# The last tile's h as seven products of halves over two of three row blocks, and its third token block ahead of the seven products of g

## The chip, the cores and the metric

The kernel runs on one core of a Trainium2 chip. The metric is device time in microseconds of one execution, from several executions. One execution was also recorded by the hardware profiler; the profile and the trace below are of that one.

The names of the engines are those of the profile. PE is TensorE's matmul and PEld its loading of weights; DVE is VectorE, ACT ScalarE, POOL GpSimd, SP the engine that issues most transfers. Every engine works through its own queue in order and waits at an instruction until the semaphores it names have come.

## What is computed

A recurrent attention (RWKV6) over 4 batches, 8 heads, 768 positions and 48 channels, whose output is taken as 3072 tokens of 384 channels, and then a feed-forward block with exact gelu:

```
for t in range(S):
    cur = einsum('bhd,bhe->bhde', u * k_t, v_t)
    y[:, :, t] = einsum('bhd,bhde->bhe', r_t, state + cur)
    state = w_t[..., None] * state + einsum('bhd,bhe->bhde', k_t, v_t)

x = y as (3072, 384)
h = x @ w_in              # w_in  (384, 2048)
g = 0.5 * h * (1 + erf(h / sqrt(2)))
out = g @ w_out           # w_out (2048, 384)
```

All is fp32. The change concerns only the feed-forward block, and of it the last 384 tokens.

## The kernel before

**Tiles.** The 3072 tokens are eight tiles of T = 384, numbered x = 0 to 7. For each, `attention(x, ...)` makes `xT`, the tile's input with channels on the partitions (three row blocks of 128 channels, 384 tokens wide), and `mlp(x)` makes the output from it. Both are generators: each `yield` is a step. The main loop runs the steps of `mlp(x - 1)` and, at steps listed by hand in `place` and `place_next`, lets the attention of tile x go on; `times` lists the steps at which loads are issued, and `more` is a generator of extra vector work of which each step takes one part. Instructions stand on each engine's queue in the order in which the code issues them. After the loop, `mlp(7)` runs alone: no attention, no load and no other step is beside it.

**h.** In `mlp`, for each of the 16 blocks f of 128 columns of `w_in`, three matmuls (L726), one for each row block j, add up a 128 x 384 block of h in a PSUM tile `h_ps`, of which there are two in turn. ScalarE applies gelu (L729) and writes the block into a `g` tile in SBUF. Where `waits` holds (x = 1, 3, 5), the last 128 tokens go into `alone` instead (L731).

**The output.** For x > 0 (`halves`) the order of the groups of f is 0, 2, 1, 3. The first two token blocks of 128 are done by seven products of halves: g over two token blocks and two halves of f, `w_out` over two halves of f and two of its columns, so that eight products of 128 x 1024 by 1024 x 192 become seven. The sums of `w_out` are made once by `w_sums` (`sums`), those of g in the last group of f by VectorE (L739, L740, L741: `s1`, `s2`, `s3`). Each product is eight matmuls of 192 columns (L746) into one of two PSUM tiles in turn, `o1` and `o2`; ScalarE or VectorE empties each (L777 to L807). The third token block of an odd tile waits in `alone` and is done with the third block of the next even tile, likewise by seven products (L816 to L851). The last tile, x = 7, has no next one, so its third block is done plainly, 16 matmuls of 384 columns (L860), after its seven products:

```python
            for blocks in ((2,),) if halves else ((0, 1), (2,)):
                o_ps = [ps.tile([128, BANK], F32, name="o_ps", tag="mm", bufs=2)[:, 0:DM] for _ in blocks]
```

VectorE copies it (L866) and SP stores it.

**PSUM.** `h_ps`, `o_ps` and `warm` share the tag "mm", two tiles of one bank. The attention has the tag "d": three tiles `[128, 2, BANK]`, each of two banks of 512 fp32.

**The attention beside it.** In tiles x >= 2 it begins with chains on VectorE (L339 to L390); then `quarters` lays out copies of r (`plain` by ScalarE, L488; `lay_out` by VectorE, L493 and L494), which 48 small matmuls read (L508, then L515). It does so twice, for 4 and for 16. Then come the states (L610, L615), the outputs `y_ps` (L630, L648) and the copies into `xT` (L672, L679). The buffers `kx`, `tot_sb`, `bufs[0]`, `bufs[1]` and `v_in` that the change uses again belong to this part.

Of the kernel before, what the change touches and what calls it, by code (L numbers as in the profile page):

```python
# [10 lines left out]
F32 = mybir.dt.float32  # L11
# [5 lines left out]
AF = mybir.ActivationFunctionType  # L17
# [6 lines left out]
T = 384  # L24
# [7 lines left out]
BANK = 512  # L32
# [12 lines left out]
def kernel(  # L45
# [25 lines left out]
    nc = tc.nc  # L71
    NX = rkw.shape[0]
    NP = u.shape[1]
    NPART = NP // Q
    N_TOK, DM = out.shape
    HALVES = 2
    NJ = DM // 128
    DF = w_in.shape[1]
    NF = DF // 128
# [4 lines left out]
    io = ctx.enter_context(tc.tile_pool(name="io", bufs=2))  # L84
    wk = ctx.enter_context(tc.tile_pool(name="wk", bufs=2))
    cv = ctx.enter_context(tc.tile_pool(name="cv", bufs=HALFWAY))
    gp = ctx.enter_context(tc.tile_pool(name="gp", bufs=4))
    ps = ctx.enter_context(tc.tile_pool(name="ps", bufs=1, space=PSUM))
# [11 lines left out]
    bufs = [io.tile([128, 3 * NP * T], F32, name=f"rkw{i}", bufs=1) for i in range(2)]  # L100
    ALL = NP * T
# [46 lines left out]
    w_out_sb = const.tile([128, NF, DM], F32, name="w_out_sb")  # L148

    WI = PIECE // NJ  # L150
    FP = PIECE // DM
    FI = WI // 128
    w_in_sb = const.tile([128, DF // WI, NJ, WI], F32, name="w_in_sb")
# [68 lines left out]
    kx = const.tile([128, 2 * NPART * NI * 3 * C // 2], F32, name="kx")  # L222
# [7 lines left out]
    for i, h in enumerate(QUARTERS):  # L230
        for a in range(3):
            w_q = (3 - a) * C // 4
            z = q_ints[1 if a == 0 else 2]
            o = i * C if a < 2 else i * C + C // 2
# [26 lines left out]
    tot_sb = const.tile([128, NP * T], F32, name="tot_sb")  # L261
# [50 lines left out]
    xT_of = {}  # L312
# [372 lines left out]
    HF, HM = NF // 2, DM // 2  # L685
    FG = 4
    sums, s3_sb = [], []
# [4 lines left out]
    def w_sums():  # L692
# [3 lines left out]
        for i, (x, y) in enumerate((((0, 1), (0, 0)), ((1, 1), 0), ((1, 1), (0, 1)), ((1, 0), 1))):  # L696
            for k in range(2):
                ks = slice(k * FG, (k + 1) * FG)
                nc.vector.tensor_sub(sums[i][:, ks], w_quarter(*x, k), sums[y][:, ks] if isinstance(y, int) else w_quarter(*y, k))
                yield  # L700

    def mlp(x):

        xT = xT_of.pop(x)
        halves = x > 0
        waits, ends = x % 2 == 1 and x < NX - 1, x % 2 == 0 and x > 0
        gs = {}
# [7 lines left out]
        def new_sums(tag):  # L717
            return cv.tile([128, FG, 128], F32, name="s", tag=tag)

        s1, s2, s3 = [], [], []  # L720
        for n, group in enumerate((0, 2, 1, 3) if halves else range(4)):
            gs[group] = gp.tile([128, FG, T], F32, name="g")
            for f in range(group * FG, (group + 1) * FG):
                h_ps = ps.tile([128, BANK], F32, name="h_ps", tag="mm", bufs=2)[:, 0:T]
                for j in range(NJ):
                    nc.tensor.matmul(h_ps, lhsT=w_in_sb[:, f // FI, j, f % FI * 128:(f % FI + 1) * 128], rhs=xT[:, j, :],  # L726
                                     start=(j == 0), stop=(j == NJ - 1))
                t = T - 128 if waits else T
                nc.scalar.activation(out=gs[group][:, f % FG, 0:t], in_=h_ps[:, 0:t], func=AF.Gelu)  # L729
                if waits:  # L730
                    nc.scalar.activation(out=alone[:, f], in_=h_ps[:, t:], func=AF.Gelu)  # L731

                if halves and n == 3 and f % FG >= FG - 2:
                    k = f % FG - FG + 2
                    for s, tag in ((s1, "f"), (s2, "e")):
                        s.append(new_sums(tag))
                    s3.append(s3_sb[0][:, k * FG:(k + 1) * FG])
                    a00, a10, a11 = (gs[g][:, :, a:a + 128] for g, a in ((k, 0), (k, 128), (k + 2, 128)))
                    nc.vector.tensor_add(s1[k], a10, a11)  # L739
                    nc.vector.tensor_sub(s2[k], s1[k], a00)  # L740
                    nc.vector.tensor_sub(s3[k], a00, a10)  # L741
                yield

        def product(o, lhs, rhs, start=False):
            for j in range(HF):
                nc.tensor.matmul(o, lhsT=lhs(j), rhs=rhs(j), start=start and j == 0, stop=(j == HF - 1),  # L746
                                 skip_group_check=True)
# [10 lines left out]
        def of_alone(b):  # L758
            return lambda j: alone[:, b * HF + j]
# [4 lines left out]
        def psum():  # L764
            return ps.tile([128, BANK], F32, name="o_ps", tag="mm", bufs=2)[:, 0:HM]

        def two_rows():
            return [wk.tile([128, DM], F32, name="o_sb", bufs=2) for _ in range(2)]


        if halves:
            row0 = x * T
            o_sb = two_rows()
            p1, u2, u3 = (wk.tile([128, HM], F32, name=name, bufs=1) for name in ("p1", "u2", "u3"))
# [21 lines left out]
            for c in range(2):  # L796
                z = o_sb[1][:, c * HM:(c + 1) * HM]
                nc.vector.tensor_add(z, z, u3)
            store(row0 + 128, o_sb[1])
            if ends:  # L800
                s1 = [new_sums("f") for k in range(2)]
# [7 lines left out]
            if ends:  # L809
                s2 = [new_sums("e") for k in range(2)]  # L810
# [5 lines left out]
        if waits:  # L816
            _, o2, o1 = psum(), psum(), psum()
            o_sb = wk.tile([128, DM], F32, name="o_sb", bufs=2)
            product(o2, of_alone(0), of_w(0, 0), True)
            nc.scalar.copy(out=p1_alone, in_=o2)  # L820
            yield
            product(o1, of_alone(1), of_w(1, 0), True)
            nc.vector.tensor_add(o_sb[:, 0:HM], o1, p1_alone)
            store(row0 + 256, o_sb[:, 0:HM])
            yield
        elif ends:
            o_sb = two_rows()
            p1, u2, u3 = p1_alone, *(wk.tile([128, HM], F32, name=name, bufs=1) for name in ("u2", "u3"))
            o2, o1 = psum(), psum()
            product(o1, of_blocks(2, 1), of_t(3), True)  # L830
            nc.scalar.copy(out=o_sb[1][:, 0:HM], in_=o1)
            yield
            product(o2, of_sums(s2), of_t(1), True)
            nc.vector.tensor_add(u2, o2, p1)
            yield
            product(o1, of_sums(s1), of_t(0), True)
            nc.scalar.copy(out=o_sb[1][:, HM:], in_=o1)
            for k in range(2):
                nc.vector.tensor_sub(s2[k], alone[:, HF + k * FG:HF + (k + 1) * FG], s2[k])
            yield  # L840
            product(o2, of_sums(s3), of_t(2))
            nc.vector.tensor_add(u3, o2, p1)
            for c in range(2):
                z = o_sb[1][:, c * HM:(c + 1) * HM]
                nc.vector.tensor_add(z, z, u3)
            store(row0 + 256, o_sb[1])
            yield
            product(o1, of_sums(s2), of_w(1, 1))
            nc.vector.tensor_add(o_sb[0][:, 0:HM], o1, u2)
            store(row0 - T + 256, o_sb[0][:, 0:HM], HM)  # L850
            yield  # L851
        else:

            if halves:
                psum()
            for blocks in ((2,),) if halves else ((0, 1), (2,)):
                o_ps = [ps.tile([128, BANK], F32, name="o_ps", tag="mm", bufs=2)[:, 0:DM] for _ in blocks]
                for f in range(NF):
                    for i, o in zip(blocks, o_ps):
                        nc.tensor.matmul(o, lhsT=block(i, f // HF, f % HF), rhs=w_out_sb[:, f, :],  # L860
                                         start=(f == 0), stop=(f == NF - 1))
                    if (not halves or f % 4 == 3) and f < NF - 1:
                        yield
                for i, o in zip(blocks, o_ps):
                    o_sb = wk.tile([128, DM], F32, name="o_sb", bufs=2)
                    nc.vector.tensor_copy(out=o_sb, in_=o)  # L866
                    store(x * T + i * 128, o_sb)
                yield
# [35 lines left out]
    for x in range(1, NX):  # L904

        place = [1, 3, 5, 7, 9, 11, 13, 15, 18, 20, 26, 32] if x == 1 else [1, 6, 8, 13, 15, 16, 18, 18, 20, 21]
        place_next = [38, 47] if x == 1 else [21, 24] if x % 2 == 0 else [25, 27]
        loads = load(x + 1, nc.scalar if x > 1 else nc.sync)

        times = range(20, 30) if x == 1 else (2, 3, 4, 5, 16, 17, 18, 19, 20, 21)  # L910
        following = attention(x + 1, 0) if x + 1 < NX else iter(())
        more = iter(())
        for step, _ in enumerate(mlp(x - 1)):
            if x == 1 and step == 2 * NF - 2:

                make_quarter_masks()
                more = w_sums()
            next(more, None)
            if x == 1 and step in (0, 2, 4, 6, 8, 10, 12, 14, 15, 17, 18, 20, 22, 24):
                convert()  # L920
            if step in times:
                next(loads, None)
            while place and place[0] <= step:
                place.pop(0)
                next(slots, None)
            while place_next and place_next[0] <= step:
                place_next.pop(0)
                next(following, None)
        for _ in slots:
            pass  # L930
        slots = following
# [62 lines left out]
```

## Time and profile before

| | us |
|---|---|
| executions | 611.08, 608.43, 612.21; median 611.08 |
| profiled execution, own time | 609.14 |
| its span, first to last instruction | 607.3 |

The last tile's `mlp` takes the last 63 us of the span. From the trace:

| part of the last tile | engine, line | records | us each |
|---|---|---|---|
| h | PE L726, 384 columns | 96 | 0.49 |
| gelu | ACT L729, 384 columns | 16 | 0.49 |
| sums of g | DVE L739 to L741, 512 columns | 6 | 0.69 |
| seven products | PE L746, 192 columns | 112 | 0.33 |
| adds from PSUM | DVE L786, L795, L807, 192 columns | 3 | 0.36 |
| copies from PSUM | ACT L777, L780, L783, L789, 192 columns | 4 | 0.32 |
| third block | PE L860, 384 columns | 32 | 0.49 |

How to read it: a matmul of the code appears as two records. A record is longer than the distance to the next, since matmuls are pipelined, so times of many are taken from the chain of waits, and not from count times mean. "Idle before" is time in which an engine stood still ahead of a group, with the instruction that ended it.

### The profile page before, as it was taken

What the parts mean: (1) busy time and instruction counts of PE and PEld (TensorE: products, weight loads), DVE (VectorE), ACT (ScalarE), POOL (GpSimd) and SP (SyncE); (2) the same over time, 40 slices, a digit from 0 to 9 for tenths busy, and PEclk for the clock granted to TensorE, in tenths of its full rate; (3) what the DMA queues carried; (4) which work ended last, traced back from release to release, by engine and by line L of the source; (5) the groups of instructions that cost most, each with busy time, mean ns of one, the idle gap of its engine ahead of it and who ended that gap; (6) DMA issues with size and microseconds to landing.
All of it is one profiled execution on the core that took longest, in us unless ns stands there. A gap on an engine that the chain in (4) does not pass through costs nothing.

```text
span 607.3 us, 15828 instructions
## 1 busy us (share of the span) xinstructions
PE 594.4 (98%) x6934; PEld 445.9 (73%) x6934; DVE 448.5 (74%) x801; ACT 173.4 (29%) x389; POOL 8.4 (1%) x24
## 2 busy tenths in 40 slices
PE   8879999999999999999999999999999999999997
PEld 4556666556698569986699568986699568995694
DVE  8969999998875978588885988679785988520120
ACT  2346376023222322213222232213222232112200
POOL 3100000000000000000000000000000000000000
PEclk9999999999999999999999999999999999999999
DMA  5767358012042305203052304203052002010001
GB/s 198 244 205 229 107 158 301 32 35 77 12 103 76 91 2 109 73 21 92 1 111 73 98 1 89 86 28 91 3 111 71 8 2 40 22 37 0 1 1 40
DMA packets 50565, 46.71 MB, mean 77 GB/s; under 512 B 31680, under 2 KB 35904, under 8 KB 50496
## 3 DMA queue, kind: packets, MB, share of 16 engines
q1 hardware_dynamic: 33152, 29.31, 15.8%
q10 hardware_dynamic: 17344, 16.39, 9.9%
q8 instruction: 55, 0.90, 0.6%
q14 instruction: 14, 0.11, 0.1%
HBM read 36.24 MB, written 4.72 MB: 67 GB/s over the span
## 4 chain that ended last, share of the span: by engine, by line
PE 86%; DVE 10%; issue 2%; ACT 1%; DVEq 0%
PE h_ps L726 37%; PE o_ps L746 31%; PE d L515 4%; PE o_ps L860 4%; DVE rkw L437 2%; PE kv_ps L592 2%; PE y_ps L648 2%; DVE e L306 2%; PE y_ps L630 2%; PE d L402 2%; PE warm L190 2%; DVE w_out_sb L310 1%; DVE a_sb L447 1%; PE d L508 1%; DVE f L303 1%
## 5 line engine op out<-in xcount | busy, mean ns | idle before, releaser
L726 PE MATMUL h_ps<-xT,w_in_sb 128*128 128x384 f32 x768 | 254.1, 489 | 1.4 <-ACT f L291 1.4
L726 PEld LDWEIGHTS h_ps<-xT,w_in_sb 128*128 128x128 f32 x768 | 144.1, 190 | 98.5 <-ACT f L291 1.9
L729 ACT ACTIVATE g<-h_ps 128x384 f32<-128x384 f32 (+1 forms) x128 | 57.3, 449 | 197.9 <-PE h_ps L726 197.9
L746 PE MATMUL o_ps<-t,s 128*128 128x192 f32 x480 | 81.9, 329 | 0.0
L746 PEld LDWEIGHTS o_ps<-t,s 128*128 128x128 f32 x480 | 77.8, 190 | 0.7
L546 DVE COPY_PREDICATED a_sb<-quarter,d 128x384 f32<-128x384 uint8 (+2 forms) x108 | 45.0, 438 | 2.5
L860 PE MATMUL o_ps<-w_out_sb,g 128*128 128x384 f32 x128 | 43.2, 491 | 0.2
L746 PE MATMUL o_ps<-w_out_sb,g 128*128 128x192 f32 x224 | 38.7, 326 | 0.0
L746 PEld LDWEIGHTS o_ps<-w_out_sb,g 128*128 128x128 f32 x224 | 37.0, 190 | 1.9
L860 PEld LDWEIGHTS o_ps<-w_out_sb,g 128*128 128x128 f32 x128 | 23.7, 190 | 17.1 <-DVE w_out_sb L310 1.4
L739 DVE TENSOR_TENSOR s<-g 128x512 f32<-128x512 f32 x14 | 9.4, 670 | 29.1 <-ACT g L729 29.1
L746 PE MATMUL o_ps<-w_out_sb,s 128*128 128x192 f32 x160 | 28.3, 330 | 0.0
L746 PE MATMUL o_ps<-t,g 128*128 128x192 f32 x160 | 27.6, 326 | 0.0
L402 PEld LDWEIGHTS d<-rkw 64*64 64x64 f32 x1152 | 18.6, 134 | 12.1 <-DVE rkw L437 7.4
L339 DVE TRANSPOSE_TENSOR_REDUCE rkw<-kx 128x48 f32<-128x1536 f32 (+3 forms) x24 | 26.8, 1154 | 0.2
L515 PEld LDWEIGHTS d<-kx,rkw 64*64 64x64 f32 x1152 | 24.3, 133 | 3.4 <-DVE a_sb L553 1.6
L515 PE MATMUL d<-kx,rkw 64*64 64x96 f32 x1152 | 26.5, 245 | 0.0
L746 PEld LDWEIGHTS o_ps<-t,g 128*128 128x128 f32 x160 | 26.3, 190 | 0.0
L746 PEld LDWEIGHTS o_ps<-w_out_sb,s 128*128 128x128 f32 x160 | 25.9, 190 | 0.4
L528 DVE TENSOR_TENSOR rkw<-rkw,tot_sb 128x768 f32<-128x768 f32 x12 | 11.5, 958 | 17.5 <-PE d L515 17.5
L402 PE MATMUL d<-rkw 64*64 64x64 f32 (+1 forms) x1152 | 21.0, 221 | 3.2 <-DVE rkw L437 2.3
L375 DVE TENSOR_TENSOR rkw<-rkw 128x384 f32<-128x384 f32 (+2 forms) x24 | 23.6, 1002 | 0.4
(117 smaller groups left out, 645.1 us busy)
## 6 DMA issues: line engine op xcount, KB each, us to landing
rkw<-in_rkw_dram ACTq DMA_DIRECT2D x45, 256.0 KB, 2.8
raw<-in_w_out_dram SPq DMA_DIRECT2D x8, 768.0 KB, 4.4
out_dram<-o_sb SPq DMA_DIRECT2D x21, 192.0 KB, 1.9
raw<-in_w_in_dram SPq DMA_DIRECT2D x5, 768.0 KB, 5.9
v_in<-in_v_dram ACTq DMA_DIRECT2D x5, 584.0 KB, 3.7
raw<-in_w_in_dram SPq DMA_DIRECT2D x9, 256.0 KB, 3.4
rkw<-in_rkw_dram SPq DMA_DIRECT2D x8, 288.0 KB, 3.9
rkw<-in_rkw_dram SPq DMA_DIRECT2D x9, 256.0 KB, 7.3
```

The source lines that it names most:

```text
L190: nc.tensor.matmul(t, lhsT=zeros[:, 0:128], rhs=zeros, start=True, stop=True)
L306: nc.vector.scalar_tensor_tensor(out=e, in0=hi, scalar=0x80000000, in1=e, op0=ALU.bitwise_and, op1=ALU.bitwise_or)
L339: nc.vector.tensor_reduce(out=fine_sb[:, e, 0:n].rearrange("p a n -> p (a n)"), in_=kx[:, o:o + n * n_m].rearrange("p (m j) -> p m j", j=3 ...
L375: nc.vector.tensor_mul(z, z, by)
L402: nc.tensor.matmul(d[half[p], g, n * width:(n + 1) * width], lhsT=kc[half[g], b, i, p], rhs=right(half[g], b, i, p), start=True, stop=True)
L437: nc.vector.tensor_mul(rk, rk, tt)
L515: nc.tensor.matmul(d[half[p], g, i * 3 * C // 2:(i + 1) * 3 * C // 2], lhsT=kc[half[g], (n + i) // NI, (n + i) % NI, p], rhs=rx[half[g], 2 ...
L546: nc.vector.copy_predicated(out=an[:, :, :, :, (a + 1) * h:], mask=mask.to_broadcast(data.shape), data=data)
L726: nc.tensor.matmul(h_ps, lhsT=w_in_sb[:, f // FI, j, f % FI * 128:(f % FI + 1) * 128], rhs=xT[:, j, :], start=(j == 0), stop=(j == NJ - 1))
L729: nc.scalar.activation(out=gs[group][:, f % FG, 0:t], in_=h_ps[:, 0:t], func=AF.Gelu)
L746: nc.tensor.matmul(o, lhsT=lhs(j), rhs=rhs(j), start=start and j == 0, stop=(j == HF - 1), skip_group_check=True)
L860: nc.tensor.matmul(o, lhsT=block(i, f // HF, f % HF), rhs=w_out_sb[:, f, :], start=(f == 0), stop=(f == NF - 1))
```

## The change

For the last tile alone, three things are different.

1. **h by seven products.** A generator `h_sums` makes four sums of `w_in` (`in_s`, each 128 x 1024, in two halves of 512) and four differences of `xT` (`in_t`, each 128 x 192), on VectorE, in the steps 2, 3, 4, 5, 17, 19, 22, 23, 24 and 26 of `mlp(6)`. They lie in buffers that the attention no longer needs: `bufs[0]`, a `v_in` buffer, `kx`, `bufs[1]`, `tot_sb`. Then `h_halves` makes the blocks f and f + 8 of h together, over two token halves of 192 and the first two row blocks, by seven products of 128 x 128 by 128 x 192; the third row block is added plainly, four matmuls of 192. Six PSUM accumulators lie in the three "d" tiles, one in each bank. VectorE puts the results together (`u2`, `u3`, `u5`, `c12`, `c21`, `c22`), and ScalarE's gelu writes four pieces of 192.
2. **The sums of g** (now `of_g`, one operation a step) are spread over the following pairs.
3. **The third token block** comes ahead of the seven products, with the blocks f = 7 and 15 last, and ScalarE copies it.

Tiles 0 to 6 issue the same instructions as before, apart from the ten steps of `h_sums`.

```diff
+    def h_sums():
+        n = DF // 2
+        rest = io.tile([128, v.shape[2]], F32, name="v_in")
+        for z in (bufs[0][:, 0:n], rest[:, 0:n], kx[:, 0:n], bufs[1][:, ALL:ALL + n]):
+            in_s.append(z.rearrange("p (i c) -> p i c", c=WI))
...
+        for i in range(4):
+            for k in range(2):
+                if i == 0:
+                    nc.vector.tensor_add(s(1, k), w(1, 0, k), w(1, 1, k))
+                elif i == 1:
+                    nc.vector.tensor_sub(s(2, k), s(1, k), w(0, 0, k))
+                elif i == 2:
+                    nc.vector.tensor_sub(s(3, k), w(0, 0, k), w(1, 0, k))
+                else:
+                    nc.vector.tensor_sub(s(4, k), w(0, 1, k), s(2, k))
+                yield
+        in_t.extend(tot_sb[:, i * HT:(i + 1) * HT] for i in range(4))
...
+        nc.vector.tensor_sub(in_t[0], x01, x00)
+        nc.vector.tensor_sub(in_t[1], x11, in_t[0])
+        yield
+        nc.vector.tensor_sub(in_t[2], x11, x01)
+        nc.vector.tensor_sub(in_t[3], x10, in_t[1])
+        yield
...
+        def h_halves():
+            banks = [ps.tile([128, 2, BANK], F32, name="d", tag="d", bufs=3) for _ in range(3)]
+            b_1, b_6, b_7, b_5, b_4, b_0 = (z[:, i, 0:HT] for z in banks for i in range(2))
...
+                multiply(b_1, (w(0, 0), x00))
+                nc.scalar.copy(out=p1, in_=b_1)
+                multiply(b_6, (s(2), in_t[1]))
+                nc.vector.tensor_add(u2, b_6, p1)
+                multiply(b_7, (s(3), in_t[2]))
+                nc.vector.tensor_add(u3, b_7, u2)
+                multiply(b_5, (s(1), in_t[0]))
+                nc.vector.tensor_add(u5, b_5, u3)
+                multiply(b_1, (w(0, 1), x10), (w(0, 2), last[0]), start=False)
+                gelu(0, 0, b_1)
+                multiply(b_4, (w(1, 1), in_t[3]), (w(1, 2), last[0]))
+                nc.vector.tensor_add(c21, b_4, u3)
+                gelu(1, 0, c21)
+                multiply(b_0, (w(1, 2), last[1]))
+                nc.vector.tensor_add(c22, b_0, u5)
+                gelu(1, 1, c22)
+                multiply(b_5, (s(4), x11), (w(0, 2), last[1]), start=False)
+                nc.vector.tensor_add(c12, b_5, u2)
+                gelu(0, 1, c12)
+                next(more, None)
+                if f % FG == FG - 1:
+                    more = of_g(k)
...
+        if final:
+            o_ps = ps.tile([128, BANK], F32, name="o_ps", tag="mm", bufs=2)[:, 0:DM]
+            order = [f for f in range(NF) if f % HF < HF - 1] + [HF - 1, NF - 1]
+            for n, f in enumerate(order):
+                nc.tensor.matmul(o_ps, lhsT=block(2, f // HF, f % HF), rhs=w_out_sb[:, f, :], start=(n == 0), stop=(n == NF - 1))
+            o_sb = wk.tile([128, DM], F32, name="o_sb", bufs=2)
+            nc.scalar.copy(out=o_sb, in_=o_ps)
+            store(x * T + 256, o_sb)
+            yield
...
-        else:
-
-            if halves:
-                psum()
-            for blocks in ((2,),) if halves else ((0, 1), (2,)):
+        elif not final:
+
+            for blocks in (0, 1), (2,):
...
-            next(more, None)
+            if x == NX - 1 and step == 2:
+                more = h_sums()
+            if x < NX - 1 or step in (2, 3, 4, 5, 17, 19, 22, 23, 24, 26):
+                next(more, None)
```

`multiply` issues one matmul for each pair of factors into the same accumulator, the first of them overwriting unless `start=False`; `gelu(a, b, z)` writes row half a and token half b of the pair's block of g.

More of the change, by code (lines that the diff above doesn't have):

```diff
@@ L700, in w_sums, with w, s @@
                 yield
+    HT = T // 2
+    in_s, in_t = [], []
+    def h_sums():
[3 more added lines that the diff above has]
+            in_s.append(z.rearrange("p (i c) -> p i c", c=WI))
+        hi = DF // WI // 2
+        def w(a, c, k):
+            return w_in_sb[:, a * hi + k * hi // 2:a * hi + (k + 1) * hi // 2, c, :]
+        def s(i, k):
+            return in_s[i - 1][:, k * hi // 2:(k + 1) * hi // 2]
+        for i in range(4):
[10 more added lines that the diff above has]
+        in_t.extend(tot_sb[:, i * HT:(i + 1) * HT] for i in range(4))
+        xT = xT_of[NX - 1]
+        x00, x01, x10, x11 = (xT[:, c, b * HT:(b + 1) * HT] for c in range(2) for b in range(2))
+        nc.vector.tensor_sub(in_t[0], x01, x00)
[4 more added lines that the diff above has]
+        yield
     def mlp(x):
@@ L718, in new_sums, with of_g @@
             return cv.tile([128, FG, 128], F32, name="s", tag=tag)
+        def of_g(k):
+            for s, tag in ((s1, "f"), (s2, "e")):
+                s.append(new_sums(tag))
+            s3.append(s3_sb[0][:, k * FG:(k + 1) * FG])
+            a00, a10, a11 = (gs[g][:, :, a:a + 128] for g, a in ((k, 0), (k, 128), (k + 2, 128)))
+            nc.vector.tensor_add(s1[k], a10, a11)
+            yield
+            nc.vector.tensor_sub(s2[k], s1[k], a00)
+            yield
+            nc.vector.tensor_sub(s3[k], a00, a10)
+            yield
@@ new lines, in h_halves, with w, s, multiply @@
+        def h_halves():
+            banks = [ps.tile([128, 2, BANK], F32, name="d", tag="d", bufs=3) for _ in range(3)]
+            b_1, b_6, b_7, b_5, b_4, b_0 = (z[:, i, 0:HT] for z in banks for i in range(2))
+            temps = [bufs[1][:, 2 * ALL + i * HT:2 * ALL + (i + 1) * HT] for i in range(8)]
+            x00, x01, x10, x11 = (xT[:, c, b * HT:(b + 1) * HT] for c in range(2) for b in range(2))
+            more = iter(())
+            for f in range(HF):
+                k = f // FG
+                if f % FG == 0:
+                    for group in (k, k + 2):
+                        gs[group] = gp.tile([128, FG, T], F32, name="g")
+                p1, u2, u3 = (wk.tile([128, HT], F32, name=name, bufs=1) for name in ("p1", "u2", "u3"))
+                u5, c12, c21, c22 = temps[f % 2::2]
+                def w(a, j):
+                    g = a * HF + f
+                    return w_in_sb[:, g // FI, j, g % FI * 128:(g % FI + 1) * 128]
+                def s(i):
+                    return in_s[i - 1][:, f // FI, f % FI * 128:(f % FI + 1) * 128]
+                def multiply(o, *factors, start=True):
+                    for i, (lhsT, rhs) in enumerate(factors):
+                        nc.tensor.matmul(o, lhsT=lhsT, rhs=rhs, start=start and i == 0, stop=(i == len(factors) - 1),
+                                         skip_group_check=True)
+                def gelu(a, b, z):
+                    nc.scalar.activation(out=gs[2 * a + k][:, f % FG, b * HT:(b + 1) * HT], in_=z, func=AF.Gelu)
+                last = [xT[:, 2, b * HT:(b + 1) * HT] for b in range(2)]
+                multiply(b_1, (w(0, 0), x00))
[20 more added lines that the diff above has]
+                    more = of_g(k)
+            for _ in more:
+                pass
@@ L720, in mlp @@
         s1, s2, s3 = [], [], []
-        for n, group in enumerate((0, 2, 1, 3) if halves else range(4)):
+        final = x == NX - 1
+        if final:
+            h_halves()
+        for n, group in enumerate(() if final else (0, 2, 1, 3) if halves else range(4)):
             gs[group] = gp.tile([128, FG, T], F32, name="g")
@@ L733, in mlp @@
                 if halves and n == 3 and f % FG >= FG - 2:
[L734 to L741, printed above, removed]
+                    for _ in of_g(f % FG - FG + 2):
+                        pass
                 yield
@@ L768, in two_rows @@
             return [wk.tile([128, DM], F32, name="o_sb", bufs=2) for _ in range(2)]
+        if final:
+            o_ps = ps.tile([128, BANK], F32, name="o_ps", tag="mm", bufs=2)[:, 0:DM]
[5 more added lines that the diff above has]
+            store(x * T + 256, o_sb)
+            yield
         if halves:
@@ L861, in mlp @@
                                          start=(f == 0), stop=(f == NF - 1))
-                    if (not halves or f % 4 == 3) and f < NF - 1:
+                    if f < NF - 1:
                         yield
```

## The prediction

> **What bounds the kernel now.** I read the page's totals first, then the chain of waits over the last tile, then the timelines of the two places that the change touches.
>
> ```profile
> span 607.3 us, 15828 instructions
> PE 594.4 (98%) x6934; PEld 445.9 (73%) x6934; DVE 448.5 (74%) x801; ACT 173.4 (29%) x389; POOL 8.4 (1%) x24
> ```
>
> TensorE is busy nearly all the span, so what counts is the work on its queue and any hole made in it. The chain of waits from 540 us to the end (start, length, what) is TensorE alone until one last copy:
>
> ```profile
> 544.26 30.96 PE h_ps L726 x96
> 575.22 18.20 PE o_ps L746 x112
> 593.42 10.33 PE o_ps L860 x32
> 603.75 0.02 issue
> 603.77 0.56 DVE o_sb L866
> ```
>
> These are the last tile's h, its seven products, and its third token block. One matmul of the code makes two records here, so L726 costs 30.96/48 = 0.645 us for 384 columns and L746 18.20/56 = 0.325 us for 192: cost goes by columns, and halving the width loses nothing **while the queue is fed**. The waits of this stretch list none on TensorE.
>
> What a wait costs is seen at about 116 us, where the first tile's third block must wait for a copy out of its PSUM tile (timeline; the bracket is idle time and its releaser):
>
> ```profile
> 115.65 0.56 DVE L866 COPY o_sb<-o_ps 128x384 f32<-128x384 f32 x1 [0.15 <-PE o_ps L860]
> 116.26 0.19 PEld L860 LDWEIGHTS o_ps<-w_out_sb,g 128*128 128x128 f32 x1 [0.62 <-DVE o_sb L866]
> 116.69 0.49 PE L860 MATMUL o_ps<-w_out_sb,g 128*128 128x384 f32 x1
> ```
>
> The copy ends at 116.21 and the weight load starts 0.05 later. The second pass starts at 116.69; a pass of 384 columns takes 30.96/96 = 0.32, so the first one took effect at 116.37. **Restart: 0.16 us after the reader's end.** The way in: the next product starts at 577.65 and the copy of the finished one (L777) at 577.85, so a **reader starts 0.20 us after the last pass's slot**.
>
> The second place is the vector queue of the tile before, where the change puts four sums (timeline):
>
> ```profile
> 486.03 0.94 DVE L375 TENSOR_TENSOR rkw<-rkw,tot_sb 128x768 f32<-128x768 f32 x1
> 487.00 0.56 DVE L493 TENSOR_TENSOR kx<-rkw,tot_sb 128x384 f32<-128x384 f32 x1
> 487.95 0.96 DVE L494 TENSOR_TENSOR kx<-kx,tot_sb 128x768 f32<-128x768 f32 x1 [0.40 <-ACT kx L488]
> 489.51 2.21 PE L515 MATMUL d<-kx,rkw 64*64 64x96 f32 x96
> ```
>
> L494 ends at 488.91 and L515, which reads it, starts at 489.51: VectorE is only 0.6 us ahead.
>
> [...] the seven products alternate o1 and o2, with 0.0 us idle. [...] the trace has 0.69 us (L740) and 0.36 (L786). [...] In the trace, 44.2 to 47.6 us had TensorE busy for 2.27 of 3.40 us at clock 1.00.
>
> **The change, part by part.**
>
> *Arithmetic of h.* Before: 48 matmuls of 384 columns, 30.96 us. After: for each of eight pairs of row blocks 11 matmuls of 192 columns (seven for the products, four for the third row block), 88 x 0.325 = 28.6. Gain 2.4 us, if fed.
>
> *Waits inside h, the decisive part.* The six accumulators lie two and two in three PSUM tiles: (b_1, b_6), (b_7, b_5), (b_4, b_0). In the built program's list of instructions with their waits, dependences are kept by tile and not by bank: TensorE's b_6 waits for ScalarE's copy of b_1 of the same pass (p1); b_5 for VectorE's u3, which reads b_7; b_0 for c21, which reads b_4. Between b_1 and b_6 TensorE has no other work, between b_7 and b_5 none, between b_4 and b_0 none. Behind each waiting matmul the whole TensorE queue stands.
>
> Durations: ScalarE's copy of 192 is 0.32 (L777). Gelu of 192 was never run; of 128 it is 0.27, of 256 0.38 (L731, L729), so 0.33, taken as 0.35 from SBUF. VectorE's add with one PSUM input is 0.36 (L786). One pass over a pair, with zero at the end of b_1's slot:
> - The previous pair's last slot ended at -0.325. Its c12 runs from -0.125 to 0.23, its gelu from 0.27 to 0.62. The copy of p1 stands behind it on ScalarE, in order; ScalarE's copies overlap by 0.09 (L488), so it runs from 0.53 to 0.85. b_6 takes effect at 0.85 + 0.16 = 1.01. **Hole 1.01.**
> - b_6 to 1.335, b_7 to 1.66. u2 from 1.535 to 1.89, u3 behind it from 1.93 to 2.29. b_5 at 2.45. **Hole 0.79.**
> - b_5, two of b_1 and two of b_4: 1.625, to 4.075. c21 from 4.275 to 4.63. b_0 at 4.79. **Hole 0.715.**
> - b_0, two of b_5 and the next b_1: 1.3, to 6.09.
>
> So 6.09 us a pair in place of 11 x 0.325 = 3.575. Eight are 48.7; the first has no gelu ahead of its copy (its hole is 0.20+0.32+0.16 = 0.68), which takes off 0.33: 48.4 us. Against 30.96: **+17.4 us**. VectorE has six adds and at most one g sum (2.1 + 0.7 us) in 6.09 and ScalarE some 1.7, so neither limits by its load; the latencies do. Bounds: a restart between 0.05 and 0.2 and a reader's start 0.05 either way move 24 holes by up to 0.15: 3 us either way; I take the middle. From below a hole is never under zero, since TensorE has no other work.
>
> *Four weight sums (s1, s2) at steps 2 to 5 of the tile before.* On VectorE they stand between L375 and L493. Their pitch is 0.61 (L739 to L741, 508.96 and 509.56), four are 2.45. L493 then runs 489.3 to 489.9, L494 490.0 to 490.9 (the 0.40 wait for ScalarE is absorbed), and L515 can start at 491.06: **+1.55 us** on TensorE, the 0.6 of lead being eaten. All that follows on both queues moves by the same, so the second L515 (501.5) needs no more. Bounds: 0 if some lead is hidden, 2.5 if none is.
>
> *The other sums at steps 17 to 26.* s3's first (0.69) stands before L610, whose L615 must wait for kv_ps at 516.5 anyway. s3's second follows L786 and holds L792 until 522.9; its product starts at 528.4. s4 follows L812, and TensorE asks VectorE again only at 541. The four x differences of 0.36 end near 543.5, and b_7 is the first to need the last ones, at 544.9. All cost nothing here; the covers are TensorE's products from 517 to 544. If those shrank, the differences would be late first, by up to 0.7.
>
> *Third block first, g sums spread.* 16 matmuls of 384 columns in both, 10.33 us; its copy goes to ScalarE and its 192 KB store on SP's queue lies under the 18.2 us of products, with no load behind it. The last three g sums (2.0 us) hide under the third block. At the end stands L807's add of 192 (0.36) in place of L866's (0.56): **-0.2 us**, and the same kind of store after it.
>
> **Sum**: +17.4 + 1.55 - 0.2 = +18.75. On the profiled execution's own 609.14 us that is 627.9; the median of the runs shown, 611.08, is 1.9 above it, and gives 629.8. I say 629.
>
> **Rivals.**
> - *The waits don't bite* (other side): if b_6, b_5 and b_0 were released by older events, the queue is fed and the sum is -2.4 - 0.2 + 1.55 = -1.05: 608 to 610. The place is b_6's wait; the point is a hole sum of (2.4 + 0.2 - 1.55)/8 = 0.13 us a pair for no change. For it speaks that before, 0.0 us was idle in products of the same width; against it, that there a reader has eight matmuls of cover and here none. 5%.
> - *Half bites*: one hole of the three hidden and restarts cheaper, about 1.25 us a pair: 10 - 1.05 = +9, 618 to 620. For it: restart and start latencies rest on single events. 6%.
> - *The clock falls*: at half clock a pair is 7.15 + 2.5 = 9.65, eight are 77, +46 + 1.35: about 657. For it, the stage is fed 59% of the time; against it, no hole passes 1.1 us and the stretch at 44 us kept clock 1.00. 4%.
> - That the change isn't what it says is excluded by the same list: 11 matmuls of 192 columns a pair, and the third block ahead of the products.
>
> **How the numbers follow.** Main case 85%: 629, its own range 624 to 634 (holes 3 us, sums 1, and 1.9 between profile and median). To leave out no more than 2 in 10 it is widened a little to 622 to 635; the rivals at 610 and 657 stay outside. 1% of 611 is 6 us, about what these runs, 608.43 to 612.21, can tell from none. Slower by over 1%: main, the clock and most of the half case, 0.92; same 0.07; faster 0.01.
>
> **What would show it.** The h stage lasts about 48 us instead of 31, with TensorE's waits naming the copy of p1, u3 and c21, eight times each, 0.7 to 1.0 us. L515's first start moves about 1.5 us later with L494 as releaser. Third block and products stay at 10.3 and 18.2. I am wrong if h lasts under 35 us, if one of the three releasers is missing, or if the clock is below 1.00 there.

## The result and the profile after

| | before | changed |
|---|---|---|
| median of four executions, us | 611.32 | 631.06 |
| profiled execution, own time, us | 609.14 | 630.74 |
| its span, us | 607.3 | 628.9 |

The ratio is 1.0327, with a 95% interval from 1.0274 to 1.0379: the changed kernel is 3.3% slower. The forecast of 629, range 622 to 635, holds the measured 631.06.

The chain of waits of the changed kernel over one pair of row blocks (start, length, what; L822 is c12 of the pair before, L802 its gelu, L806 the copy of p1, L798 the matmul of `multiply`, L808 and L810 are u2 and u3, L816 is c21):

```profile
554.08 0.37 DVE rkw L822
554.45 0.02 issue
554.47 0.36 ACT g L802
554.83 0.22 ACT p L806
555.05 0.04 issue
555.05 0.04 issue
555.09 0.61 PE d L798 x2
555.70 0.02 issue
555.72 0.37 DVE u L808
556.09 0.03 issue
556.12 0.02 DVEq L810
556.14 0.04 issue
556.18 0.37 DVE u L810
556.55 0.04 issue
556.60 1.91 PE d L798 x10
558.50 0.02 issue
558.53 0.37 DVE rkw L816
558.89 0.04 issue
558.94 1.26 PE d L798 x6
```

In the kernel before, this stretch was one line of TensorE, 30.96 us long. Now the chain leaves TensorE three times a pair: for c12 and the gelu of the pair before and the copy of p1, then for u2 and u3, then for c21. The matmul that starts here at 555.09 starts for the next pair at 561.23, so a pair takes 6.14 us. What TensorE's weight loads waited for from 540 us on (total, times, longest):

```profile
PEld d L798 <- ACT p L806: 7.9, 8, 1.0
PEld d L798 <- DVE u L810: 7.1, 8, 0.9
PEld d L798 <- DVE rkw L816: 6.0, 8, 0.7
```

These are the three waits that the prediction named, eight times each. The rest of the last tile (chain of waits) is as long as it was, 10.3 and 18.2 us, in the other order:

```profile
595.79 1.24 PE d L798 x6
597.03 10.32 PE o_ps L882 x32
607.35 18.21 PE o_ps L853 x112
```

h begins where the last product of the tile before ends, at 532.42 + 15.80 = 548.22, and ends at 597.03: 48.81 us. The second place, in the timeline of the changed kernel:

```profile
488.76 1.27 DVE L726 TENSOR_TENSOR v_in<-rkw,w_in_sb 128x512 f32<-128x512 f32 x2
489.96 0.54 DVE L493 TENSOR_TENSOR kx<-rkw,tot_sb 128x384 f32<-128x384 f32 x1
490.60 0.96 DVE L494 TENSOR_TENSOR kx<-kx,tot_sb 128x768 f32<-128x768 f32 x1
491.82 3.86 PE L515 MATMUL d<-kx,rkw 64*64 64x96 f32 x96 [1.58 <-DVE kx L494]
```

The last two of the four sums stand ahead of L493, L494 ends too late, and TensorE waits 1.58 us for it. But the last line holds a second thing: the same 96 records took 2.21 us before and 3.86 now. The windows of 1 us around it (us, then the busy time of PE, PEld, DVE, ACT and POOL, and as the first number after these the clock that TensorE was granted, 1.00 being full speed) show why:

```profile
490.00:491.00 1.00, 0.24 (x6) 0.14 (x4) 0.90 (x3) 0.00 (x0) 0.00 (x0) 1.00 0.00 0
491.00:492.00 1.00, 0.18 (x8) 0.21 (x12) 0.90 (x2) 0.00 (x0) 0.00 (x0) 1.00 0.00 0
492.00:493.00 1.00, 1.00 (x33) 1.00 (x32) 1.00 (x1) 0.00 (x0) 0.00 (x0) 0.50 0.00 0
493.00:494.00 1.00, 1.00 (x33) 1.00 (x29) 0.03 (x1) 0.00 (x0) 0.00 (x0) 0.50 0.08 16
```

TensorE was busy for 0.42 of the two microseconds from 490 to 492. Then its clock is halved (0.50 from 492.0 to 495.4 us), and 3.4 us later it is back (0.80 over 495 to 496 us, 1.00 after). That is another 1.65 us.

So the difference of the two profiled executions, 630.74 - 609.14 = 21.6 us, is: h 48.81 - 30.96 = +17.85; L515's wait +1.6; the halved clock +1.65; the end -0.2; and +0.66 at 312 us, where the matmuls of `kv_ps` in tile 3 follow a gap of 0.98 us in place of 0.32, in a part that both kernels issue alike. Together 21.6. The last of these is hardly the change's doing: in the run below with only the third token block moved, which leaves all up to the end of h as it was, h begins at 544.95 us in place of 544.26, 0.69 us late.

### The profile page after: what moved, and what is told of

It is laid out like the page before. It is cut to its first block, busy times and chain, and to the rows that moved or that the text cites. A ratio compares the mean times of both kernels' runs of the same rounds, so it can differ in the third digit from the quotient of the medians.

```text
span 628.9 us, 16102 instructions
## 1 busy us (share of the span) xinstructions
PE 600.5 (95%) x7014; PEld 457.4 (73%) x7014; DVE 471.1 (75%) x860; ACT 179.2 (28%) x414; POOL 8.4 (1%) x24
## 4 chain that ended last, share of the span: by engine, by line
PE 81%; DVE 14%; issue 3%; ACT 2%; DVEq 0%
PE o_ps L853 29%; PE h_ps L839 28%; PE d L798 5%; PE d L515 4%; DVE rkw L437 2%; PE o_ps L976 2%; PE y_ps L648 2%; PE kv_ps L592 2%; DVE e L306 2%; PE warm L190 2%; PE d L402 2%; PE o_ps L882 2%; PE y_ps L630 2%; DVE w_out_sb L310 1%; DVE a_sb L447 1%
## 5 line engine op out<-in xcount | busy, mean ns | idle before, releaser
L839 PE MATMUL h_ps<-xT,w_in_sb 128*128 128x384 f32 x672 | 223.0, 489 | 1.4 <-ACT f L291 1.4
L839 PEld LDWEIGHTS h_ps<-xT,w_in_sb 128*128 128x128 f32 x672 | 125.9, 190 | 86.0 <-ACT f L291 1.9
L842 ACT ACTIVATE g<-h_ps 128x384 f32<-128x384 f32 (+1 forms) x112 | 49.5, 444 | 169.3 <-PE h_ps L839 169.3
L853 PEld LDWEIGHTS o_ps<-w_out_sb,g 128*128 128x128 f32 x224 | 37.0, 190 | 1.9
L976 PE MATMUL o_ps<-w_out_sb,g 128*128 128x384 f32 x96 | 32.7, 493 | 0.2
L515 PE MATMUL d<-kx,rkw 64*64 64x96 f32 x1152 | 28.2, 254 | 1.6 <-DVE kx L494 1.6
L515 PEld LDWEIGHTS d<-kx,rkw 64*64 64x64 f32 x1152 | 25.9, 140 | 5.0 <-issue 3.3
L976 PEld LDWEIGHTS o_ps<-w_out_sb,g 128*128 128x128 f32 x96 | 17.7, 190 | 13.1 <-DVE w_out_sb L310 1.4
L798 PE MATMUL d<-xT,w_in_sb 128*128 128x192 f32 x96 | 21.8, 335 | 3.6 <-DVE rkw L816 3.6
L488 ACT COPY kx<-rkw 128x384 f32<-128x384 f32 x36 | 16.1, 509 | 29.3 <-PE d L515 19.0
```

Source lines behind the costliest of these rows:

```text
L488: nc.scalar.copy(out=z, in_=r4[:, :, :, f, :])
L515: nc.tensor.matmul(d[half[p], g, i * 3 * C // 2:(i + 1) * 3 * C // 2], lhsT=kc[half[g], (n + i) // NI, (n + i) % NI, p], rhs=rx[half[g], 2 ...
L798: nc.tensor.matmul(o, lhsT=lhsT, rhs=rhs, start=start and i == 0, stop=(i == len(factors) - 1), skip_group_check=True)
```

## The experiments

**Five PSUM tiles for the accumulators.** The arithmetic, the order and the six banks' worth of accumulators stay; only who shares a tile is changed. b_6 and b_4 share one, since u2 has long read b_6 when b_4 is written.

```diff
-            b_1, b_6, b_7, b_5, b_4, b_0 = (z[:, i, 0:HT] for z in banks for i in range(2))
+            b_1, b_0 = (ps.tile([128, BANK], F32, name="h_acc", tag="mm", bufs=2)[:, 0:HT] for _ in range(2))
+            b_7, b_5, b_6 = (z[:, 0, 0:HT] for z in banks)
+            b_4 = banks[2][:, 1, 0:HT]
```

> The changed kernel with its six accumulators in five PSUM tiles instead of three (b_1 and b_0 in the two tiles of tag mm, b_7, b_5 and the pair b_6, b_4 in the three of tag d). Theory (false waits by tile): the three holes of a pair close but for some 0.05 us at b_1's second part, h falls from 48.8 us to 28.6 to 29.5, and the whole to 0 to 2.5 us above the kernel before, since the 1.6 us ahead of L515 stay. Rival (the chain p1, u2, u3, c21 itself holds TensorE, whatever the tiles): the waits only move to the next matmul that needs the results, h stays above 40 us, the whole 10 us or more above before.

Measured: 610.45 us, ratio to before 0.9999, interval 0.9981 to 1.0017. The chain of waits at the start and the end of h in that run (`h_acc` are b_1 and b_0):

```profile
547.20 0.33 PE h_acc L800 x2
547.52 0.97 PE d L800 x6
548.50 0.65 PE h_acc L800 x4
549.15 0.65 PE d L800 x4
549.80 0.33 PE h_acc L800 x2
550.12 0.65 PE d L800 x4
...
575.99 10.32 PE o_ps L884 x32
```

b_1, then b_6, b_7 and b_5 without a break, then the second part of b_1: TensorE alone. h takes 575.99 - 547.20 = 28.79 us against 48.81. The same products, sums and gelus hang on each other as before, so the chain of data doesn't hold TensorE; the sharing of tiles did, and its price was 20.0 us. What is left above the kernel before at L515 (1.6 us, and a mean clock of 0.997 or less in 11 of 20 executions) eats the 2.2 us that h gains.

**One wait at a time.** In three runs a single accumulator of the changed kernel was given a tile of its own.

```diff
-            b_1, b_6, b_7, b_5, b_4, b_0 = (z[:, i, 0:HT] for z in banks for i in range(2))
+            b_1, _, b_7, b_5, b_4, b_0 = (z[:, i, 0:HT] for z in banks for i in range(2))
+            b_6 = ps.tile([128, BANK], F32, name="h_acc", tag="mm", bufs=2)[:, 0:HT]
```

The second run does this with b_5 in place of b_6, the third with b_0.

> The changed kernel with b_6 alone taken out of b_1's tile, into a tile of tag mm; b_7, b_5 and b_4, b_0 still share theirs. Theory: b_6's wait (about 1.0 us) goes, but the copy of p1 still ends at the same time and u2, u3 behind it, so that b_5's hole grows from 0.8 to 1.2 us. A pair takes 5.5 to 5.6 us in place of 6.14, h 44 us. Rival (each hole is a cost by itself, as the sum of the prediction added them): 1.0 us a pair goes, a pair takes 5.1, h 41.

> The changed kernel with b_5 alone in a PSUM tile of its own (tag mm), so that it no longer shares one with b_7. Theory (only the place of the wait counts, and u3 is needed by nothing on TensorE until c21): b_5's hole of 0.8 us goes whole and the other two stay, a pair 5.3 to 5.4 us, h 42.5 us. Rival (as with b_6, a part of the hole comes back at b_0, which waits for c21, which needs u3): a pair above 5.6.

> The changed kernel with b_0 alone in a PSUM tile of its own (tag mm), so that it no longer shares one with b_4. Theory: b_0's hole of 0.7 us goes whole, a pair 5.4 us, h 43 us. Rival (gelu and c12 come later by as much and the copy of p1 of the next pair behind them): the hole ahead of b_6 grows and a pair stays above 5.8.

| alone in its tile | h, us | saved of 48.81 | whole, us, one execution |
|---|---|---|---|
| b_6 | 43.6 | 5.2 | 626.63 |
| b_5 | 42.5 | 6.3 | 622.56 |
| b_0 | 43.1 | 5.7 | 624.36 |
| all apart | 28.8 | 20.0 | 610.45 (median) |

The first three of the last column are single executions, with mean clocks of 0.997, 0.996 and 0.999; the saving is read from h. With b_6 apart TensorE's waits over the last tile are:

```profile
PEld d L799 <- DVE u L811: 9.0, 8, 1.2
PEld d L799 <- DVE rkw L817: 6.0, 8, 0.7
```

The wait for p1 (7.9 us) is gone, but the one for u3 has grown from 7.1 to 9.0: u3 needs u2, and u2 needs p1. With b_5 apart the other two waits keep their totals (7.9 and 6.0), with b_0 apart too (7.9 and 7.1), and the one goes whole. The first hole is worth less alone than in company (the three single gains add up to 17.2, not 20.0), as the first theory said.

**The sums alone.** The kernel before, with `h_sums` at the same steps and nothing else; their results are not used.

```diff
+            if x == NX - 1 and step == 2:
+                more = h_sums()
-            next(more, None)
+            if x < NX - 1 or step in (2, 3, 4, 5, 17, 19, 22, 23, 24, 26):
+                next(more, None)
```

> The kernel before with nothing but the twelve added sums of w_in and xT at the same ten steps; their results are not used. Theory: L515's first matmuls wait 1.6 us for L494, and in those executions in which the clock of TensorE falls in that hole, its 96 records take 3.8 us instead of 2.2: 1.6 to 3.3 us slower than before, ratio 1.0026 to 1.0055. Rival (the sums are hidden, and the wait in the changed kernel came from elsewhere): within 0.5 us of before. Rival (the sums at steps 17 to 26 cost too): over 4 us.

Measured: ratio 1.0049, interval 1.0029 to 1.0068, about 3 us. In its profiled execution (timeline) the clock did not fall at this place:

```profile
493.01 0.96 DVE L494 TENSOR_TENSOR kx<-kx,tot_sb 128x768 f32<-128x768 f32 x1
...
494.22 2.21 PE L515 MATMUL d<-kx,rkw 64*64 64x96 f32 x96 [1.57 <-DVE kx L494]
```

So the wait belongs to the sums. The later sums cost nothing that can be seen: from L515 to the start of h both kernels take 54.75 us.

Whether the clock falls at L515 is different from execution to execution. Of the six profiled executions with this hole open, L515's 96 records took 3.86 us in the changed kernel and 3.67 with b_6 apart, but 2.21 with the sums alone and with five tiles. Of the other two the mean clocks are 0.996 (b_5 apart) and 0.999 (b_0 apart). Of the four without it L515 took 2.21 us in three (the kernel before, and below the hole filled and the hole avoided), and the fourth (the third block moved) has a mean clock of 1.00.

Of the other executions only the mean clock is known. A fall of 3.4 us to one half, as in the changed kernel, makes a mean clock of 1 - 1.7/610 = 0.997. That, or less, stands in 12 of 18 executions of this kernel, in 7 of the 55 of the kernel before beside them, in 3 of 4 of the changed kernel, and in 11 of 20 of the one with five tiles, which has the hole too. The mean does not say where the clock fell: the profiled execution of this kernel has 0.997 as well, and its L515 took the 2.21 us of full speed. So only the difference in these counts between kernels with and without the hole can be put down to the hole.

**Useless work in the hole.** The same kernel, with six matmuls on zeros ahead of L515.

```diff
+                if x == NX - 1 and h == FINE:
+                    keep_warm(6)
                 ds = []
```

> The kernel with nothing but the added sums, and six matmuls on zeros (512 columns, bf16) issued ahead of L515 at that one place, 1.3 us of work of no use in a hole of 1.6. Theory (TensorE's clock falls for 3.4 us because the hole is there): the share of executions with a mean clock of 0.997 or less goes from two in three (12 of 18) to about that of before (7 of 55), L515's 96 records take 2.2 us, and the median comes down by about 1 us to ratio 1.002 to 1.004. Rival (the clock falls for another reason, such as the small matmuls themselves): the share stays at about two in three and the ratio at 1.005.

Measured: ratio 1.0027, interval 1.0015 to 1.0039; a mean clock of 0.997 or less in 0 of 15 executions. In the timeline the zeros fill the hole, and L515 (here L517) takes its 2.21 us:

```profile
488.71 1.47 PE L190 MATMUL warm<-zeros 128*128 128x512 bf16 x5
489.15 0.96 DVE L494 TENSOR_TENSOR kx<-kx,tot_sb 128x768 f32<-128x768 f32 x1
490.18 2.05 PEld L517 LDWEIGHTS d<-kx,rkw 64*64 64x64 f32 x96 [0.50 <-PE warm L190]
490.21 2.21 PE L517 MATMUL d<-kx,rkw 64*64 64x96 f32 x96
```

This fits the theory, but does not show it. The run was on another chip than the one with the sums alone, and there the kernel before has such a mean in 0 of 20 executions; the only two executions on it with the hole left open have 0.996 (b_5 apart) and 0.999 (b_0 apart). The two ratios are from two chips as well, and their intervals overlap. The stronger evidence is the last run below.

**The third block first, alone.** The kernel before, with only the third token block moved ahead of the products and copied by ScalarE.

```diff
+        if x == NX - 1:
+            o_ps = ps.tile([128, BANK], F32, name="o_ps", tag="mm", bufs=2)[:, 0:DM]
...
+            nc.scalar.copy(out=o_sb, in_=o_ps)
+            store(x * T + 256, o_sb)
+            yield
         if halves:
             row0 = x * T
```

> The kernel before with nothing but the third token block ahead of the seven products in the last tile, and its copy on ScalarE. Theory: the last thing is the add of 192 columns (0.36 us) in place of the copy of 384 (0.56): the chain's end 0.2 us shorter, no hole on TensorE between h, third block and products. Rival (the third block now stands right behind the last gelu and waits for it): a hole of 0.5 us or more ahead of its last matmul, and the end no earlier.

Measured: 609.6 us in one execution, beside a median of 609.71 for the kernel before. Its chain of waits has no hole, and ends with the shorter operation (in that run L816 is the add of L807):

```profile
575.91 10.32 PE o_ps L774 x32
586.23 18.21 PE o_ps L746 x112
604.44 0.02 issue
604.47 0.36 DVE o_sb L816
```

0.2 us is all it is worth, too little for a single time to tell.

**Both mended.** Five tiles, and the four sums moved to where VectorE had stood idle for 3.3 us, in the tile before. In the timeline of the changed kernel that place is:

```profile
471.92 0.36 DVE L941 TENSOR_TENSOR o_sb<-o_ps,rkw 128x192 f32<-128x192 f32 x1 [3.30 <-issue]
```

```diff
+            if x == NX - 2 and step == 22:
+                early = h_sums()
+                for _ in range(4):
+                    next(early)
-            if x == NX - 1 and step == 2:
-                more = h_sums()
-            if x < NX - 1 or step in (2, 3, 4, 5, 17, 19, 22, 23, 24, 26):
+            if x == NX - 1 and step == 2:
+                more = early
+            if x < NX - 1 or step in (17, 19, 22, 23, 24, 26):
                 next(more, None)
```

> As the run with five tiles, and the four sums s1 and s2 moved from steps 2 to 5 of the last but one tile's feed-forward block to step 22 of the one before it, where VectorE stands idle for 3.3 us. Theory: L515's wait and the fall of the clock go too; the sum is 29 - 31 for h and -0.2 at the end: 1.5 to 2.5 us faster than before, ratio 0.996 to 0.9975. Rival (the sums delay L371 and all behind it, so L494 is late again): L515 waits as before, ratio about 1.000.

Measured: 608.13 us, ratio 0.9955, interval 0.9939 to 0.9971: 0.45% faster than the kernel before, a little more than was expected. VectorE's queue in the timeline, and L515:

```profile
467.88 1.27 DVE L724 TENSOR_TENSOR rkw<-w_in_sb 128x512 f32<-128x512 f32 x2
469.07 1.28 DVE L726 TENSOR_TENSOR v_in<-rkw,w_in_sb 128x512 f32<-128x512 f32 x2
471.25 0.36 DVE L943 TENSOR_TENSOR o_sb<-o_ps,rkw 128x192 f32<-128x192 f32 x1 [0.90 <-issue]
...
489.50 2.21 PE L515 MATMUL d<-kx,rkw 64*64 64x96 f32 x96
```

The four sums end 0.9 us before L943 (the add of L823, L941 in the changed kernel) can start, so what stands behind it is as early as in the kernel before. L515 starts at 489.50 (489.51 before) and waits for nothing. h takes 573.02 - 544.24 = 28.78 us. A mean clock of 0.997 or less stands in 2 of 22 executions, against 11 of 20 with five tiles on the same chip, where nothing but the place of the four sums is different. So most of these low clocks come with the hole and go with it.

## Why the prediction was right

- *Waits inside h*, predicted +17.4 us, measured +17.85. The mechanism is shown: the three releasers are those named, and setting the accumulators apart takes 20.0 us back. The size was 0.05 us a pair too small. The term is the step from u2 to u3: taken as 0.04 us, it is 0.03 + 0.02 + 0.04 = 0.09 in the chain. Gelu of 192 columns, taken as 0.33 us and as 0.35 from SBUF, is 0.33 from PSUM and 0.36 from SBUF (L802).
- *Holes as a plain sum.* The prediction worked out a pair as a whole, and that came out (6.09 against 6.14). Its rival of half the cost had one of the three holes hidden; the waits show all three, eight times each, and the single runs show that the first, taken away, comes back in part at the second.
- *Arithmetic of h*, 28.6 us if fed: 28.8 in both runs with five tiles.
- *Four sums*, predicted 1.55 us at L515: 1.58 in the changed kernel, 1.57 with the sums alone.
- *What it missed*: the clock at L515. It looked for a fall inside h, where TensorE works 59% of the time, and held it unlikely; there the clock stayed at 1.00. Half speed, and holes of up to 1.1 us as too short for a fall, were its estimates: the trace of the kernel before has a clock of 1.00 throughout. It gave no thought to the hole that it had itself put ahead of L515, of 1.58 us, where a fall to 0.50 cost 1.65 us in the profiled execution. Three of the four executions have a mean clock of 0.997, but only the profiled one shows where it fell.
- *Luck in the number.* On the profiled execution the sum gave 627.9, and 630.74 was measured. The 2.8 us between are the clock (1.65), the gap at 312 us (0.66), h (0.45) and rounding. The 1.9 us that were then added to reach a median came from the kernel before; the changed kernel's median is only 0.3 us above its profiled execution. So an allowance that did not come true made up for more than half of what was missed.
- *The other sums and the third block*, nothing and -0.2 us: both as predicted, the second by the chain of waits alone.

That the waits come from dependences kept by tile was read from the list of instructions with their waits; the runs show that sharing a tile is the cause. Whether the chip itself would have allowed the unguarded accesses was not tried.

## What to carry to other kernels

Splitting a long accumulation into short products that hang on each other left no work here between a matmul and its reader: three holes of 0.7 to 1.0 us in every pair of 6.14. With each accumulator that is read while others are written in a PSUM tile of its own, or beside a partner whose reader is long done, h went from 48.81 to 28.79 us. Work out such a loop on all its engines together, for a wait taken away can come back at the next one (with p1's 7.9 us gone, u3's went from 7.1 to 9.0). Before work is put on a queue with little to do on average, look at what there has only half a microsecond of lead (0.6 us ahead of L515, where four sums of 2.4 us made TensorE wait 1.58), and put it into a wait of that queue instead (here the 3.3 us ahead of L941).

## What the runs showed of the hardware

In the profiled execution of the changed kernel TensorE's clock fell from 1.00 to 0.50 for 3.4 us, from 492.0 to 495.4 us, 0.2 us after the end of a hole of 1.58 us; it was 1.00 in the rest of that trace. The same hole was not followed by slow records every time: L515's took 3.86 us there and 3.67 with b_6 apart, but 2.21 with the sums alone (a hole of 1.57 us) and with five tiles (1.6). With the hole avoided (both mended, against five tiles) mean clocks of 0.997 or less went from 11 of 20 executions to 2 of 22.

Holes of 0.7 to 1.0 us, three in every 6.1 us, did not make it fall: the clock was 1.00 from 548.2 to 597.0 us. Nor did one of 1.41 us that ends at 45.3 us, in the trace of either kernel. In the 3.4 us before the fall TensorE was busy for 1.82 us, while the least in a stretch of 3.4 us inside h was 2.08, and around the hole at 45 us 1.99, all at 1.00. But the run with the sums alone has as long a hole after the same matmuls, and its L515 took 2.21 us. What does decide it is open; whether the small matmuls on either side of L515's hole have a part in it was not tried.
